# Linear attention and an FFT gate on one Trainium2 core: new shapes for the output transfers, bf16 inverse halves, a new order

## The chip, the core and the metric

The kernel runs on one core of a Trainium2 chip. The core has TensorE (PE) for matrix products into PSUM (8 banks of 2 KB in each of 128 partitions), VectorE (DVE), ScalarE (ACT) and GpSimd (POOL) for elementwise work, and SyncE (SP), which here issues transfers. 16 DMA engines move data between HBM and SBUF; transfers are issued from queues of SP, POOL and, at one place of the new kernel, ACT. The metric is device time in microseconds (us) of one execution.

## What is computed

Batch 8, 8 heads, sequence S = 576, head size 64, model width 512. All inputs and the output are fp32.

```python
kv  = einsum('bhsd,bhse->bhde', k, v)
o   = einsum('bhsd,bhde->bhse', q, kv)
o   = o / sqrt(mean(o*o, axis=-1) + 1e-6) * g_norm
x   = o, heads side by side                     # [8, 576, 512]
x1, x2, x3 = split(x @ w_proj, 3)               # w_proj [512, 1536]
x2_conv = irfft(rfft(x2, axis=1) * rfft(filter_fft, axis=0))   # circular, length 576
out = (x1 * x2_conv * x3) @ w_out               # [8, 576, 512]
```

## The kernel before

The work is written as small steps, each a Python function that issues a few instructions. The string `ORDER` names them one after the other as `step.batch`; each engine runs its own instructions in that order, and waits only for the data and buffers that they need. So the order of the words sets the order on every engine at once, and nothing is reordered later.

For one batch the steps are these.

- *Loads*: `Lq`, `Lk`, `Lv` fetch q, k, v and turn them to bf16 on POOL's queue, double-buffered by batch; `Lw1`, `Lw2`, `Lw3` the three parts of w_proj, `Lwo` w_out, `Lf` the filter. 96 partitions hold six consecutive rows each.
- *Attention*: q is transposed on PE (`T0`, `T1`, evacuated by `eT..`) for the first two batches, and by a DMA transpose on SP's queue (`Qt`) for the others; a tiny POOL copy `one_` then keeps a later load of q behind that transpose. `K`, `eK` make the products k'v and put them in `kvblk`; `O`, `sq`, `ob` (or `ov` on DVE), `R`, `rs` and `x` make the normed x, in 128-channel blocks j with time along the free dimension.
- *Folding and forward transform*: length 576 is split into three thirds and into even and odd parts. `fd`, `fr`, `fa` are the sums and differences of x on DVE; `rrM`, `rrT`, `abM`, `abT` multiply them by the middle third of w_proj; `err`, `eab`, `eT` evacuate to `x2`; `F0`, `F1`, `F2` are the transforms, against tables `FW`, `FX`, `FY`, `FZ`.
- *Product with the filter*: `M0`, `M1`, `M2` on DVE against `HH`, `HM`, then `A0` on POOL and `Av1` on DVE, into `Y`. The tables and `HH`, `HM` are made at the start: `Zi`, `Zt`, `An` the angles, `Tb0` to `Tb2` the transposes, `Ff0` to `Ff2` the folding of the filter, `H0` to `H2`, `HN0`, `HN1` its transform.
- *Gates*: `Ga`, `x1.` (ACT) and `Gb`, `g` (DVE) make x1*x3, four blocks each.
- *Inverse*: for two blocks at a time, `I01`, `I23` the even half and `Io01`, `Io23` the odd half, on PE. ACT copies the odd half to `os` in fp32; DVE combines the even half, straight from PSUM, with it into `u` (`u01`, `u23`). `w` undoes the thirds, `fin` multiplies with the gates into `yg`. The last batch has variants: `J2`, `J3` make whole blocks on PE with the negated table `IVN`, and its thirds are done apart.
- *Output*: `U0`, `U2` multiply two blocks of 128 times of `yg` by w_out, `U4` a block shared by two batches, `V` the last batch's; ACT (`ot0`, `ot2`, `ot4`) evacuates to an `ot` tile, and SP issues the transfers.

PSUM is used as four pairs of banks: `take` gives the pair that has been free longest, also to a step that needs one bank only, and `free` gives it back when its evacuation has been issued. A later step on the same pair waits for that evacuation.

Times are kept in a permuted order: `t_of(blk)` is the first time of a block of 32, whose 32 times lie six rows apart. In 128 partitions of an output block lie four such groups. The kernel issues one transfer for each 32 partitions, often for both blocks of an `ot` tile at once:

```python
return bass.AP(tensor=out.tensor, offset=out.offset + (b * S + t0[0]) * DM, ap=[[6 * DM, 32]] + two + [[1, DM]])
...
for i in range(4):
    nc.sync.dma_start(out=o_rows(b, 2 * (b % 2) + 4 * c0 + i, 2 * (b % 2) + 4 * c0 + 4 + i), in_=ot[32 * i:32 * i + 32])
```

Lines that matter: PE gates L585, output products L708, L721, L747, inverse L612, L613, last batch's inverse L642, L644, half-wide products L505, F2 L552, filter transform L308, L311; DVE product L560, combination L621, L622, x L457; ACT evacuations L522 (x2), L591 (gates), L616 (os), L712 (ot); POOL sum L566; SP transfers L174 (g_norm), L376 (transposes), L715, L728, L762 to L772 (outputs).

Of the kernel before, what the change touches and what calls it, by code (L numbers as in the profile page):

```python
# [19 lines left out]
ORDER = """Lq.0 Z.0 Zi.0 Lkb.0 Lka.0 Zd.0 Zt.0 Lva.0 An.0 Lvb.0 Zf.0 T0.0.18 Act.0 Tb0.0 Lf.0 eTv0.0 Lw1.0 Tb2.0 Tb1.0 Ka.0 eKa.0  # L20
Kb.0 eKb.0 Lq.1 Lw3.0 T1.0 eTv1.0 O01.0 sq1.0 sq0.0 ov1.0 ov0.0 O23.0.2 R0.0 R1.0 Lk.1 sq3.0 sq2.0 rs0.0 ov3.0 ov2.0
R2.0 Lv.1 R3.0 rs1.0 x0.0 Lw2.0 fr0.0 rs2.0 rs3.0 Ff1.0 x1.0 Ff2.0 fd1.0 fr1.0 Ff0.0 T0.1 Ga0.0 eTa0.1 x10.0 Ga2.0
fd0.0 Gb0.0 fa1.0 T1.1 g0.0 eTa1.1 x12.0 H0.0 H2.0 Lv.2 H1.0 K.1 fa0.0 Ga1.0 eK.1 x11.0 HN0.0 rrM.0 O01.1 rrT.0 sq1.1
ob1.1 Lk.2 err.0 sq0.1 abM.0 Gb2.0 ob0.1 F0.0 g2.0 eab.0 abT.0 eT.0 O23.1 F2.0 M0.0 sq2.1 ob2.1 Gb1.0 F1.0 M2.0 sq3.1
HN1.0 ob3.1 R1.1 g1.0 Lq.2 R0.1 Ga3.0 rs1.1 rs0.1 R2.1 K.2 Lq.3 A0.0 Qt.2 M1.0 R3.1 Qt.3 x13.0 rs2.1 x0.1 rs3.1 eK.2
Lk.3 Lv.3 Gb3.0 Av1.0 Io01.0 os01.0 I01.0 x1.1 O01.2 Lwo.0 g3.0 u01.0 Ga1.1 fd.1 sq1.2 Io23.0 ob1.2 R1.2 x11.1 Lv.4
Ga0.1 rs1.2 I23.0 os23.0 fa.1 abM.1 sq0.2 fr.1 x10.1 ob0.2 u23.0 w.0 eab.1 abT.1 O23.2 rrM.1 eT.1 sq3.2 R0.2 rrT.1
ob3.2 rs0.2 fin.0 F2.1 err.1 Gb1.1 sq2.2 F0.1 M2.1 Ga3.1 ob2.2 Lk.4 g1.1 R3.2 Lq.5 x13.1 Lq.4 F1.1 rs3.2 M0.1 K.3 eK.3
R2.2 M1.1 Gb3.1 rs2.2 Gb0.1 g3.1 O23.3 U0.0 sq2.3 sq3.3 x1.2 g0.1 Ga2.1 Av1.1 x0.2 A0.1 ob3.3 ot0.0 Io01.1 x12.1 fd.2
os01.1 fa.2 Gb2.1 I01.1 Io23.1 ob2.3 u01.1 g2.1 Lv.5 abM.2 I23.1 os23.1 abT.2 u23.1 eab.2 eT.2 Ga0.2 x10.2 O01.3 K.4  # L30
Ga1.2 Qt.4 sq0.3 fr.2 ob0.3 eK.4 sq1.3 rrM.2 x11.2 F1.2 w.1 rrT.2 R2.3 ob1.3 err.2 Gb0.2 rs2.3 fin.1 M1.2 F0.2 U2.0
R3.3 g0.2 rs3.3 Gb1.2 M0.2 F2.2 A0.2 ot2.0 g1.2 R0.3 M2.2 R1.3 Ga2.2 rs1.3 Ga3.2 x1.3 rs0.3 x0.3 x12.2 O23.4 Lq.6
x13.2 sq2.4 Av1.2 Gb2.2 ob2.4 U4.1 Lk.5 sq3.4 fd.3 ob3.4 g2.2 ot4.1 U0.1 fa.3 fr.3 Qt.5 R3.4 Io01.2 ot0.1 os01.2 abT.3
rs3.4 I01.2 eT.3 u01.2 Gb3.2 Io23.2 g3.2 os23.2 I23.2 abM.3 u23.2 eab.3 O01.4 rrM.3 F1.3 sq0.4 w.2 ob0.4 sq1.4 rrT.3
err.3 M1.3 U2.1 ob1.4 F0.3 Ga1.3 R1.4 fin.2 ot2.1 x11.3 Ga0.3 Gb0.3 M0.3 R0.4 A0.3 rs1.4 x10.3 Av1.3 F2.3 Lv.6 rs0.4
g0.3 Gb1.3 Zn.0 R2.4 M2.3 rs2.4 g1.3 Lk.6 K.5 Io01.3 I01.3 x1.4 os01.3 x0.4 eK.5 Ga2.3 x12.3 u01.3 Ga3.3 O23.5 Io23.3
x13.3 os23.3 sq3.5 ob3.5 U0.2 ot0.2 fd.4 I23.3 sq2.5 ob2.5 fa.4 Gb2.3 u23.3 Lk.7 g2.3 abM.4 O01.5 fr.4 eab.4 abT.4
Gb3.3 Qt.6 sq0.5 eT.4 ob0.5 sq1.5 rrM.4 g3.3 R3.5 rrT.4 rs3.5 err.4 K.6 F1.4 eK.6 Ga1.4 ob1.5 R0.5 Ga0.4 x11.4 w.3
F0.4 rs0.5 x10.4 fin.3 M1.4 M0.4 F2.4 R1.5 U2.2 rs1.5 Gb1.4 R2.5 M2.4 ot2.2 A0.4 g1.4 Ga3.4 O23.6 rs2.5 x13.4 sq2.6
x1.5 Av1.4 ob2.6 Gb0.4 sq3.6 Gb3.4 ob3.6 g0.4 g3.4 Ga2.4 x12.4 U4.3 x0.5 O01.6 Io01.4 fd.5 ot4.3 sq0.6 U0.3 os01.4  # L40
ob0.6 fr.5 sq1.6 I01.4 Gb2.4 ob1.6 u01.4 Lq.7 rrM.5 Io23.4 Lv.7 ot0.3 R0.6 g2.4 I23.4 rrT.5 os23.4 rs0.6 K.7 fa.5
u23.4 R1.6 abT.5 err.5 abM.5 rs1.6 w.4 R3.6 Qt.7 eT.5 eK.7 eab.5 F0.5 Ga1.5 rs3.6 R2.6 F1.5 x11.5 fin.4 F2.5 rs2.6
M0.5 U2.3 M1.5 A0.5 ot2.3 Ga0.5 x10.5 M2.5 Gb1.5 x1.6 g1.5 Av1.5 O23.7 sq2.7 Gb0.5 Ga2.5 ob2.7 sq3.7 g0.5 Ga3.5 x0.6
x12.5 ob3.7 fd.6 I01.5 fa.6 Gb2.5 Io01.5 x13.5 g2.5 U0.4 Io23.5 os01.5 Ga0.6 u01.5 ot0.4 fr.6 os23.5 I23.5 abM.6 u23.5
abT.6 x10.6 Gb3.5 eab.6 O01.7 eT.6 Ga1.6 w.5 g3.5 sq1.7 F1.6 ob1.7 fin.5 x11.6 sq0.7 rrM.6 R0.7 rrT.6 ob0.7 rs0.7 M1.6
F2.6 R1.7 err.6 M2.6 Gb0.6 rs1.7 F0.6 g0.6 U0.5 R2.7 M0.6 Ga2.6 x0.7 rs2.7 R3.7 x12.6 Gb1.6 Gb2.6 A0.6 ot0.5 rs3.7
Av1.6 g1.6 Ga3.6 g2.6 Io01.6 x1.7 fr.7 I01.6 x13.6 Gb3.6 os01.6 g3.6 Io23.6 u01.6 U2.4 ot2.4 rrM.7 fd.7 fa.7 Ga0.7
I23.6 os23.6 u23.6 x10.7 rrT.7 err.7 abM.7 Ga1.7 w.6 eab.7 abT.7 F0.7 Gb0.7 x11.7 eT.7 Gb1.7 F2.7 fin.6 M0.7 g0.7 F1.7
A0.7 U2.5 M2.7 M1.7 ot2.5 U0.6 Gb2.7 ot0.6 Av1.7 Io01.7 g1.7 I01.7 os01.7 J2.7 uj2.7 Ga2.7 x12.7 u01.7 Ga3.7 w01.7
x13.7 J3.7 g2.7 fin01.7 Gb3.7 uj3.7 wo23.7 U4.5 g3.7 fo23.7 Vp0.7 ot4.5 wm23.7 U4a.7 Vp2.7 Vq0.7 U4b.7 vap0.7 fm23.7  # L50
vau.7 dsp01.7 vvp1.7 Vq2.7 U2.6 dgp12.7 vaq0.7 dgp13.7 vvq1.7 dsp10.7 dgp03.7 dsu0.7 dsu1.7 dsq01.7 dsp00.7 dgu2.7
dsq00.7 dgq02.7 dgp02.7 dsp11.7 dgq03.7 ot2.6 dgu3.7"""
# [769 lines left out]
```

## Time and profile before

| | |
|---|---|
| three runs, median | 223.71 us (221.02 to 224.76) |
| span of the profiled execution | 218.7 us |
| PE busy | 203.8 us, 93% |
| DVE busy | 187.8 us, 86% |
| ACT busy | 147.6 us, 68% |
| POOL busy | 52.0 us, 24% |
| mean granted TensorE clock | 0.993 |
| moved by DMA | 30.12 MB, 138 GB/s |
| output transfers | 68 from `U_ev` and `U4_ev`, 16 for the last blocks |

The span runs from the first to the last instruction of one profiled execution; the median of the separately timed runs is 5.0 us above it. Busy time is the union of an engine's instructions; consecutive matmuls overlap in it, and their ends are modelled. A line of groups reads: source line, engine, operation, output and inputs, shapes, count, then busy us and mean ns, then the idle time ahead of it and what ended it. In the rows on transfers, q0 is POOL's queue and q1 the queue of SP (and of ACT); a packet is what one DMA engine moves at a time.

### The profile page before, as it was taken

How to read it: one execution, taken by the hardware profiler on the slowest of the kernel's cores; microseconds unless marked ns; L12 is line 12 of the kernel's file. 1: busy time of each engine (PE TensorE's matmuls, PEld its weight loads, DVE VectorE, ACT ScalarE, POOL GpSimd, SP SyncE). 2: the span in 40 equal slices, each digit the busy share in tenths (PEclk: the TensorE clock that was granted, in tenths of full speed). 3: DMA queues.
4: the chain of work that ended last, by engine and by line, in shares of the span. 5: the costliest groups of instructions: out<-in, count | busy, mean ns of one | idle time of the engine just before them, and what ended most of it. 6: DMA issues, size and time to landing. Idle time of an engine off the chain costs nothing.

```text
span 218.7 us, 4569 instructions
## 1 busy us (share of the span) xinstructions
PE 203.8 (93%) x1829; PEld 123.3 (56%) x1829; DVE 187.8 (86%) x277; ACT 147.6 (68%) x231; POOL 52.0 (24%) x61
## 2 busy tenths in 40 slices
...
GB/s 41 184 212 202 204 205 204 205 185 71 194 201 204 240 169 63 161 209 180 100 103 199 229 1 165 216 162 27 96 31 67 0 89 34 74 1 167 66 159 188
DMA packets 41032, 30.12 MB, mean 138 GB/s; under 512 B 15986, under 2 KB 36466, under 8 KB 41010
## 3 DMA queue, kind: packets, MB, share of 16 engines
...
HBM read 33.69 MB, written 9.44 MB: 197 GB/s over the span
## 4 chain that ended last, share of the span: by engine, by line
PE 70%; DVE 15%; ACT 7%; POOL 3%; issue 2%; POOLq 0%; DVEq 0%; ACTq 0%
PE ps L585 24%; PE ps L708 10%; PE ps L512 5%; PE ps L612 4%; DVE tpw L560 3%; PE ps L518 2%; PE ps L498 2%; PE ps L429 2%; PE ps L351 2%; PE ps L552 2%; POOL Y L566 2%; PE ps L422 2%; PE ps L544 2%; PE ps L747 2%; PE ps L545 2%
## 5 line engine op out<-in xcount | busy, mean ns | idle before, releaser
L585 PE MATMUL ps<-x,wp 128*128 128x288 bf16 x512 | 71.0, 286 | 0.2
L585 PEld LDWEIGHTS <-wp 128*128 128x128 bf16 x512 | 48.8, 98 | 17.3 <-issue 2.0
L566 POOL TENSOR_TENSOR Y<-tpw 97x1024 bf16<-97x1024 f32 x8 | 21.4, 2670 | 67.7 <-DVE tpw L560 67.7
L560 DVE TENSOR_TENSOR tpw<-ps,HH 97x2048 f32<-97x2048 f32 (+1 forms) x16 | 36.4, 2286 | 1.0 <-PE ps L537 0.4
L443 ACT ACTIVATE rstd<-ps,bias_eps 128x576 bf16<-128x576 f32 x32 | 23.3, 748 | 8.8 <-PE ps L429 8.3
L593 DVE TENSOR_TENSOR g<-ps,x 128x576 bf16<-128x576 f32 x32 | 24.1, 752 | 5.3 <-ACT o L439 3.5
L591 ACT CAST x<-ps 128x576 bf16<-128x576 f32 x32 | 20.5, 640 | 9.4 <-PE ps L585 6.1
L708 PE MATMUL ps<-wo,yg 128*128 128x512 bf16 x112 | 26.3, 379 | 0.0
L522 ACT CAST x<-ps 128x1024 bf16<-128x1024 f32 (+1 forms) x24 | 20.8, 874 | 6.4 <-PE ps L512 4.8
L432 ACT ACTIVATE sq<-ps 128x576 bf16<-128x576 f32 x32 | 20.7, 661 | 2.6 <-PE ps L422 2.6
L712 ACT COPY ot<-ps 128x1024 f32<-128x1024 f32 x12 | 12.2, 1017 | 13.3 <-PE ps L708 13.2
L439 ACT ACTIVATE o<-ps,g_col 128x576 bf16<-128x576 f32 x28 | 21.1, 755 | 0.0
L708 PEld LDWEIGHTS <-yg 128*128 128x128 bf16 x112 | 10.5, 97 | 12.2 <-issue 0.6
L377 POOL COPY one__100<-qT 1x2 bf16<-1x2 bf16 x6 | 2.0, 329 | 64.3 <-DMA qT<-qb 64.3
L612 PE MATMUL ps<-IV,Y 128*128 128x192 bf16 x120 | 15.7, 246 | 0.3 <-DVE Y L566 0.3
L512 PE MATMUL ps<-wp,ab 128*128 128x512 bf16 x64 | 15.1, 379 | 0.0
L621 DVE TENSOR_TENSOR u<-ps,os 128x576 bf16<-128x576 f32 x15 | 11.3, 755 | 3.3 <-PE ps L613 2.3
L616 ACT COPY os<-ps 128x576 f32<-128x576 f32 x15 | 9.6, 641 | 6.1 <-PE ps L613 3.2
L429 PE MATMUL ps<-sq,ind 128*128 128x288 bf16 x64 | 12.6, 286 | 1.1 <-DVE o L437 0.9
L457 DVE TENSOR_TENSOR x<-o,rstd 128x1152 bf16<-128x1152 bf16 x16 | 12.8, 812 | 0.3 <-ACT rstd L443 0.3
L613 PE MATMUL ps<-IV,Y 97*128 97x96 bf16 x60 | 12.4, 207 | 0.2 <-POOL Y L566 0.2
L612 PEld LDWEIGHTS <-Y 128*128 128x128 bf16 x120 | 9.5, 98 | 3.3 <-DVE Y L566 0.6
...
## 6 DMA issues: line engine op xcount, KB each, us to landing
out_dram<-ot SPq DMA_DIRECT2D x50, 128.0 KB, 2.4
...
kb<-in_k_dram POOLq DMA_DIRECT2D x7, 576.0 KB, 11.1
vb<-in_v_dram POOLq DMA_DIRECT2D x7, 576.0 KB, 12.1
wp<-in_moe_w_proj_dram POOLq DMA_DIRECT2D x3, 512.0 KB, 16.6
...
```

The costliest lines, as they stand in the source:

```text
L432: act.activation(out=halves(sq()[:, j]), in_=tmp['o', b, j][:, :, 0:TH], func=AF.Square)
L439: act.activation(out=by_time(osb(), j), in_=i_, func=AF.Copy, scale=g_col)
L443: act.activation(out=by_time(rstd(), j), in_=by_row(tmp['r', b, j]), func=AF.Abs_reciprocal_sqrt, scale=1.0 / D, bias=bias_eps)
L512: nc.tensor.matmul(pp[:, h], abt()[:, j, 2 * h * P:(2 * h + 1) * P], w2(j), start=(j == 0), stop=(j == NDC - 1))
L522: act.copy(out=o_(), in_=tmp[key, b])
L560: vec.tensor_mul(out=t_[:n], in0=xp[:n].unsqueeze(1).to_broadcast([n, 2, 2, DM]), in1=two)
L566: op(out=Yt()[:n, 2 * g:2 * g + 2], in0=t_[:n, ::-1, 0], in1=t_[:n, ::-1, 1])
L585: nc.tensor.matmul(pp[:, h, 0:TH], w_, x[:, j, h * TH:(h + 1) * TH], start=(j == 0), stop=(j == NDC - 1))
L591: act.copy(out=x1, in_=pp[:, :, 0:TH])
L593: vec.tensor_mul(out=halves(g13t()[:, dc]), in0=pp[:, :, 0:TH], in1=x1)
L612: nc.tensor.matmul(pp[:, i, 0:SB], Y[:, 2 * g + h, cs], IV[:, 2 * g + h, 0:SB], start=(g == 1), stop=(g == 2))
L708: nc.tensor.matmul(pp[:, cc], ygt(b)[:, dc, b % 2 * 64 + c * P:b % 2 * 64 + (c + 1) * P], wo[:, dc], start=(dc == 0), stop=(dc == NDC - 1))
```

## The change

- *Outputs.* `t_of` now counts the times of a third in another order (`blk % 6` in place of `blk % 6 // 3 + 2 * (blk % 3)`), so that the four groups of 32 in a block of 128 follow each other by one row. A block whose four groups lie in one third is written by one transfer of 128 partitions, and every third block, which crosses into the next third, by two transfers of 64. `ot` tiles rotate by a table. The last batch has no special transfers; one of its transfers is issued by ACT.
- *Inverse.* ACT evacuates both halves, even and odd, in bf16 into one tile `eo` (`es`, `os`); DVE combines them in SBUF, for all four blocks at once, except in the last batch. `J2`, `J3` and `IVN` are no longer used.
- *Filter transform on full rows.* The third row block of `ff` and `FW` is filled up with zeros, and `H2`'s table is used for both halves at once: six matmuls in place of twelve. The angles are computed with fewer steps, the absolute value on DVE.
- *F2.* Three full matmuls become two pairs of half-wide ones (`FV`).
- *Single banks.* `take` manages eight banks; a step that needs one takes one.
- *Transpose.* POOL's wait for a DMA transpose is a step of its own, `Qh`.
- *Order.* `ORDER` is another string.

```diff
-ORDER = """Lq.0 Z.0 Zi.0 Lkb.0 Lka.0 Zd.0 Zt.0 Lva.0 An.0 Lvb.0 Zf.0 T0.0.18 Act.0 Tb0.0 Lf.0 eTv0.0 Lw1.0 Tb2.0 Tb1.0 Ka.0 eKa.0
+ORDER = """Z.0 W.0.16 Lqa.0 Zi.0 Zt.0 An.0 Zd.0 Zf.0 T0.0 eTv0.0 Zz.0 Tb2.0 Tb1.0 Tb0.0 Lf.0 Ff1.0 Ff0.0 Ff2.0 Lvb.0 Lkb.0 Kb.0
...
-        i = min(range(4), key=lambda x: seen[x])
+        idle = [x for x in range(8) if seen[x] is not None]
+        if n == 2:
+            i = min((x for x in idle if x % 2 == 0 and x + 1 in idle), key=lambda x: max(seen[x], seen[x + 1]))
+        else:
+            i = min(idle, key=lambda x: (x ^ 1 in idle, seen[x]))
...
-        return SB * (blk // 6) + blk % 6 // 3 + 2 * (blk % 3)
+        return SB * (blk // 6) + blk % 6
...
-                m = P if a < 2 else 32
-                kw = dict(start=(a == 0), stop=(a == 2))
-                if g < 2:
-                    nc.tensor.matmul(hp[:n, ri], FW[:m, a, 2 * g + ri, 0:n], ff[:m, a, ri], **kw)
-                else:
-                    for dup in range(2):
-                        nc.tensor.matmul(hp[dup * NM:(dup + 1) * NM, ri], FW[:m, a, 4 + ri, ri * NM:(ri + 1) * NM], ff[:m, a, ri], **kw)
+                nc.tensor.matmul(hp[:n, ri], FW[:, a, 2 * g + ri, 0:n], ff[:, a, ri], start=(a == 0), stop=(a == 2))
...
     def by_time(t, j):
-        return t[:, j].rearrange("p (m a r) -> p a m r", m=3, a=2)
+        return t[:, j].rearrange("p (m a r) -> p a m r", m=9, a=2)
...
-        for i in range(3):
-            mm(xp, FZ[:, 2 + i], x2[:, 2 + i], start=(i == 0), stop=(i == 2))
+        for c, t_ in ((lo, FW[:, 0, 4, lo]), (hi, FV)):
+            mm(xp[c], t_, x2[:, 2 + c.start // 64], start=True, stop=False, tile_position=(0, c.start))
+        for c in (lo, hi):
+            mm(xp[c], FZ[:, 2, c], x2[:, 4], start=False, stop=True, tile_position=(0, c.start))
...
-    def inv_os(b, d0):
-        act.copy(out=buf("os", 0, [P, 2, TH], FP32), in_=tmp['i', b, d0, 1][:, :, 0:TH])
-        free(("i", b, d0, 1))
-
-    def inv_u(b, d0):
-        p_, os_, u = tmp['i', b, d0, 0][:, :, 0:TH], buf("os", 0, [P, 2, TH], FP32), ut()[:, d0:d0 + 2]
-        vec.tensor_add(out=u[:, :, 0:TH], in0=p_, in1=os_)
-        vec.tensor_sub(out=u[:, :, TH:S], in0=p_[:, :, ::-1], in1=os_[:, :, ::-1])
-        free(("i", b, d0, 0))
+    eo = lambda: buf("eo", 0, [P, 2, NDC, TH])
+
+    def inv_ev(b, d0, h):
+        act.copy(out=eo()[:, h, d0:d0 + 2], in_=tmp['i', b, d0, h][:, :, 0:TH])
+        free(("i", b, d0, h))
+
+    def inv_u(b, d0, n):
+        e_, o_ = (eo()[:, h, d0:d0 + n] for h in range(2))
+        u = ut()[:, d0:d0 + n]
+        vec.tensor_add(out=u[:, :, 0:TH], in0=e_, in1=o_)
+        vec.tensor_sub(out=u[:, :, TH:S], in0=e_[:, :, ::-1], in1=o_[:, :, ::-1])
...
+    def o_rows(b, g, n=1):
+        return bass.AP(tensor=out.tensor, offset=out.offset + (b * S + SB * (g // 3) + 2 * (g % 3)) * DM,
+                       ap=[[DM, 2 * n], [6 * DM, 32], [1, DM]])
+
+    def o_dma(q, b, blk, t):
+        if blk % 3 != 2:
+            q.dma_start(out=o_rows(b, blk, 2), in_=t)
+        else:
+            for i, r in enumerate((lo, hi)):
+                q.dma_start(out=o_rows(b, blk + i), in_=t[r])
...
     def U_ev(b, c0):
-        ot = ot_tile(b)
+        ot = ot_tile(b, c0)
         act.copy(out=ot, in_=tmp['u', b, c0])
         free(("u", b, c0))
-        for i in range(4):
-            nc.sync.dma_start(out=o_rows(b, 2 * (b % 2) + 4 * c0 + i, 2 * (b % 2) + 4 * c0 + 4 + i), in_=ot[32 * i:32 * i + 32])
+        for i in range(2):
+            o_dma(nc.sync, b, b % 2 + 2 * (c0 + i), ot[:, i])
...
+    def V(b, c):
+        for h in range(1 if c < 3 else 2):
+            n = DM if c < 3 else DM // 2
+            tmp['v', c, h] = take(("v", c, h), 1)
+            for dc in range(NDC):
+                nc.tensor.matmul(tmp['v', c, h][:, 0:n], ygt(b)[:, dc, 64 + c * P:64 + (c + 1) * P], wo[:, dc, h * n:(h + 1) * n],
+                                 start=(dc == 0), stop=(dc == NDC - 1))
```

What the change moves on the queues is seen in the built programs' orders (line, operation, output and input, shape of the output). On SP's queue, the last rows before, from the last transpose on; `ot`, `sq`, `o` and `rstd` are the tiles that hold output blocks:

```order
L376 DMA_TRANSPOSE qT<-qb_75 128x24x96
L715 DMA out_dram<-ot 32x2x512 x2
L715 DMA out_dram<-ot 64x1x512 x4
L715 DMA out_dram<-ot 32x2x512 x12
L715 DMA out_dram<-ot 64x1x512 x2
L715 DMA out_dram<-sq 64x1x512 x2
L715 DMA out_dram<-sq 32x2x512 x2
L728 DMA out_dram<-ot 32x512 x4
L762 DMA out_dram<-ot 32x512 x2
L772 DMA out_dram<-o 32x512 x2
```

The same place after the change:

```order
L714 DMA out_dram<-ot 4x32x512
L717 DMA out_dram<-ot 2x32x512 x2
L714 DMA out_dram<-ot 4x32x512 x3
L717 DMA out_dram<-ot 2x32x512 x2
L714 DMA out_dram<-o 4x32x512 x2
L714 DMA out_dram<-sq 4x32x512
L717 DMA out_dram<-sq 2x32x512 x2
L717 DMA out_dram<-rstd 2x32x512 x2
L714 DMA out_dram<-ot 4x32x512
L717 DMA out_dram<-ot 2x32x512 x2
L714 DMA out_dram<-ot 4x32x512
```

Transfers of 32 partitions and two blocks, or 32 partitions, have become transfers of 128 partitions with an outer size of 4, and pairs of 64 partitions with an outer size of 2; the number of rows of 2 KB is the same.

On ACT, around the first inverse after batch 1's k'v (`x` is a gate or an x2 evacuation, `rstd`, `sq`, `o` the attention), before:

```order
L591 CAST x_564<-ps_67 128x576
L443 ACTIVATE rstd<-ps_68,bias_eps 128x2x3x96
L616 COPY os<-ps_69 128x576
L432 ACTIVATE sq<-ps_66 128x576
L591 CAST x_427<-ps_67 128x576
L439 ACTIVATE o<-ps_66,g_col 128x2x3x96
L522 CAST x_586<-ps_69 128x1024
```

and after:

```order
L608 CAST x_661<-ps_66 128x576
L635 CAST eo<-ps_69 128x576
L635 CAST eo<-ps_67 128x576
L608 CAST x_582<-ps_66 128x576
L635 CAST eo<-ps_69 128x576
L608 CAST x_661<-ps_67 128x576
L635 CAST eo<-ps_66 128x576
```

ACT now has four evacuations of the inverse where it had two (the second `os` comes further down), and they stand close together.

On POOL's queue, the first loads before (`kb`, `vb`, `qb` with two buffers each, `fn` the filter, `wp` the parts of w_proj in the order w1, w3, w2):

```order
L120 DMA qb_74<-in_q_dram 96x8x384
L178 ISA
L178 IOTA ki 128x1
L180 IOTA tvi 128x384
L120 DMA kb_70<-in_k_dram 96x4x384 x2
masks.py:197 MEMSET ident 128x128
masks.py:199 AFFINE_SELECT ident<-ident 128x128
L120 DMA vb_72<-in_v_dram 96x4x384 x2
L278 DMA fn<-in_moe_filter_fft_dram 96x3072
L129 DMA wp<-in_moe_w_proj_dram 128x4x512
L120 DMA qb_75<-in_q_dram 96x8x384
```

and after, from the filter on (the first half of q stands ahead of it; `wp` comes as w2, w1, w3):

```order
L298 DMA fn<-in_moe_filter_fft_dram 96x3072
L126 DMA vb_72<-in_v_dram 96x4x384
L126 DMA kb_70<-in_k_dram 96x4x384 x2
L126 DMA vb_72<-in_v_dram 96x4x384
L126 DMA qb_74<-in_q_dram 96x4x384
L126 DMA qb_75<-in_q_dram 96x8x384
L126 DMA kb_71<-in_k_dram 96x8x384
L126 DMA vb_73<-in_v_dram 96x8x384
L135 DMA wp<-in_moe_w_proj_dram 128x4x512
L126 DMA vb_72<-in_v_dram 96x8x384
L135 DMA wp<-in_moe_w_proj_dram 128x4x512
```

The filter now comes second, and the first part of w_proj after batch 1's q, k and v.

232 lines of the change are left out of this document (107 added, 125 removed).

## The prediction

> **What bounds the kernel now.** I read the page first, then the engines stretch by stretch, then the tail in order of time, then the transfers.
>
> ```profile
> span 218.7 us, 4569 instructions
> PE 203.8 (93%) x1829; PEld 123.3 (56%) x1829; DVE 187.8 (86%) x277; ACT 147.6 (68%) x231; POOL 52.0 (24%) x61
> ```
>
> The stretches (columns: PE, weight loads, DVE, ACT and POOL busy, granted clock, transfer share, GB/s) say where:
>
> ```profile
> 24.00:30.00 6.00, 6.00 (x53) 3.68 (x50) 5.00 (x12) 2.56 (x4) 0.77 (x1) 1.00 1.31 203
> 60.00:80.00 20.00, 19.93 (x235) 12.83 (x232) 19.47 (x25) 14.88 (x27) 3.12 (x2) 1.00 1.34 212
> 100.00:120.00 20.00, 20.00 (x194) 12.63 (x193) 18.23 (x22) 16.26 (x26) 5.71 (x5) 1.00 0.78 137
> 140.00:160.00 20.00, 20.00 (x191) 13.10 (x189) 19.40 (x24) 14.14 (x22) 2.54 (x2) 1.00 0.55 104
> 180.00:200.00 20.00, 20.00 (x142) 12.36 (x140) 18.89 (x24) 8.65 (x11) 2.36 (x1) 1.00 0.24 59
> 212.00:218.70 6.70, 0.00 (x0) 0.00 (x0) 0.00 (x0) 0.00 (x0) 1.19 (x3) 0.79 0.66 196
> ```
>
> From about 24 to 209 us TensorE never waits, with DVE close behind (18.2 to 19.5 of 20 us). Work taken from DVE or put on ACT is therefore hidden, as long as PE stays fed. The tail is different:
>
> ```profile
> 209.01 1.89 PE L708 MATMUL ps<-wo,yg 128*128 128x512 bf16 x8
> 212.75 0.58 SPq L762 DMA_DIRECT2D out_dram<-ot  x1
> 213.43 2.25 SPq L715 DMA_DIRECT2D out_dram<-rstd  x4
> ```
>
> The last matmul ends at 210.9 and the span 7.8 us later: SP is still issuing transfers until 215.7, about 0.6 us each, and 3.0 us pass from its last issue to the end.
>
> **The transfers, seen closely.** SP's first transfers and what its queue (q1) moved in the first 40 us, in which g_col is its only transfer:
>
> ```profile
> 0.74 0.73 SPq L174 DMA_DIRECT2D g_col<-in_g_norm_dram  x1
> 42.89 6.70 SPq L376 DMA_TRANSPOSE qT<-qb  x2
> ```
> ```profile
> q1 hardware_dynamic: 130, 0.00, 0.1%
> g_col<-in_g_norm_dram SPq DMA_DIRECT2D x1, 0.5 KB
> ```
>
> And from 176 to 190 us, when only outputs move (slices of 0.35 us):
>
> ```profile
> GB/s 0 0 0 0 0 0 41 217 193 193 252 375 199 100 0 0 0 0 0 0 0 0 0 0 0 0 70 205 199 187 281 351 193 12 0 0 0 0 0 0
> DMA packets 642, 1.07 MB, mean 77 GB/s; under 512 B 128, under 2 KB 128, under 8 KB 640
> q1 hardware_dynamic: 640, 1.05, 29.3%
> out_dram<-ot SPq DMA_DIRECT2D x8, 128.0 KB, 2.2
> ```
>
> Eight outputs of 128 KB are 512 packets of 2 KB, and 128 tiny ones are left over: 16 a transfer. g_col is 128 elements of 4 bytes in 130 packets: 2 left over. I read the tiny packets as completions, one from each DMA engine that worked: 16 engines carry an output, 2 carried g_col. The pattern fits the shapes: an output's outermost dimension is 32 rows in both source and target, while g_col's source is [2, 64]. The width is then the largest number up to 16 that divides both outermost sizes.
>
> The new outputs are written as `[[DM, 2n], [6*DM, 32], [1, DM]]`: outermost 4 with 128 partitions on the other side, or 2 with 64. By this reading they run on 4 engines or on 2, where the old ones ran on 16. The Trainium skill, "DMA: Bandwidth & Descriptors", section "Why a DMA increments its semaphore by 16 and not by 1", states the same rule (the largest count up to 16 that divides the slowest dimension of both patterns, and on this queue the lowest-numbered engines); the trace agrees with its counts, 16 and 2, and no row here shows which engines. By that rule the sum is the one I forecast; without it the sum is the first rival's.
>
> **The change, part by part.**
>
> *PE work.* Rows of the chain, in order of time:
>
> ```profile
> 29.34 1.79 PE ps L311 x12
> 80.07 0.55 PE ps L505 x4
> 85.56 0.66 PE ps L552 x3
> 199.38 0.33 PE ps L642 x4
> ```
> ```profile
> L612 PE MATMUL ps<-IV,Y 128*128 128x192 bf16 x120 | 15.7, 246 | 0.3 <-DVE Y L566 0.3
> L311 PE MATMUL ps<-ff,FW 128*64 128x512 bf16 x8 | 1.2, 391 | 0.0
> ```
>
> H2 goes from twelve half-wide matmuls (1.79) to six of 0.66/3 = 0.22: -0.5. F2 goes from three full ones (0.66) to four half-wide like L505 (0.55), eight times: -0.9. The last batch's J2, J3 (four groups like L642, 1.32, and eight small ones) become half as many: -0.8. Sum -2.2, all on the path, since PE is the path.
>
> *DVE and ACT.*
>
> ```profile
> L621 DVE TENSOR_TENSOR u<-ps,os 128x576 bf16<-128x576 f32 x15 | 11.3, 755 | 3.3 <-PE ps L613 2.3 <-ACT os L616 0.8
> L457 DVE TENSOR_TENSOR x<-o,rstd 128x1152 bf16<-128x1152 bf16 x16 | 12.8, 812 | 0.3 <-ACT rstd L443 0.3
> L616 ACT COPY os<-ps 128x576 f32<-128x576 f32 x15 | 9.6, 641 | 6.1 <-PE ps L613 3.2 <-DVE u L622 2.7
> ```
>
> The four half-batch combinations from PSUM (0.755 each, 3.0 a batch) become two over 1152 bf16 elements, priced like L457 (0.81): -1.4 a batch, -11 in all. ACT gains two evacuations of 0.64 a batch, +10. Both lie under PE: 0 to the sum. If PE's cover is gone, ACT's 16.3 of 20 us (100 to 120) becomes 17.5 and still fits. The 32-element runs that `by_time` and `by_row` now have are in no row; between 0 and 0.1 us on 64 evacuations, off the path: 0.
>
> *The start.* Loads land at 203 GB/s (row 24 to 30), 2.9 us for 576 KB, one behind the other.
>
> ```profile
> 8.93 0.54 PEld L385 LDWEIGHTS <-qb 96*128 96x128 bf16 x12 [0.79 <-DMA qb<-in_q_dram]
> 24.04 3.11 PE L585 MATMUL ps<-x,wp 128*128 128x288 bf16 x24
> 29.38 1.11 ACT L319 ACTIVATE hu<-ps,cf 97x1024 f32<-97x1024 f32 x1 [0.30 <-PE ps L308]
> 30.53 1.41 DVE L324 SCALAR_TENSOR_TENSOR HH<-ps,cf,hu 97x512 f32<-97x512 f32 x2 [1.46 <-ACT hu L319]
> 36.50 1.90 PE L512 MATMUL ps<-wp,ab 128*128 128x512 bf16 x8
> ```
>
> The first q landed at 8.9, so the stream began near 6.0. w1 used to end the first 2.9 MB of it (about 20) and now ends 5.8 MB, at 6.0 + 28.4 = 34.4: the gates of batch 0, which began at 24.0, begin ten us later. In exchange the filter transform and the attention come first. Their DVE chain, added up: the last fold is evacuated near 14.2, then eKb and Zc (1.7), hu of H1 at 16.6, three pairs of L324 (4.2), kvblk and three qT copies (2.6), four `ov` (3.0), and x, fr, fd, fa of batch 0 (6.1): 32.5, after which abM.0 can run, which ran at 36.5. One part is later and the other earlier; adding PE's pieces in both orders, I find about 24.5 us of work behind it at 42 us either way. I take 0, with -5 (PE does all that the loads allow) and +3 (every hand-over between engines late) as bounds. The split Qt/Qh only lets POOL issue loads while a transpose is under way: 0.
>
> *Outputs.* 68 issues by `U_ev` and `U4_ev` and 16 at the end become 48, so SP no longer holds the tail; if they kept 16 engines, about 5.5 us would pass from the last matmul to the end instead of 7.8: -2.3. But on 4 or 2 engines each of the 48 puts 32 packets of 2 KB on the busiest engine, where an old 128 KB transfer put 4. The best slice above, 375 GB/s over 16 engines, is 87 ns a packet; the loads' 203 GB/s of bf16 reads twice that in fp32, which as a rate is 80 ns; the 29.3% of 16 engines over 14 us, over 512 packets, is 128 ns. I take 87, from the densest stream of outputs: 2.8 us a transfer. That the engines are the same ones each time is my choice; no row shows it.
>
> Now the queue. Behind U2.4 the order has 24 transfers and, by the pieces above (14 gates at 0.98, five U at 1.73, six single blocks at 0.86, the inverses and transforms of batches 6 and 7), 38.7 us of PE work. The transfers need 24 x 2.8 = 67 us. PE would end at 210.9 - 2.2 = 208.7, so U2.4 is evacuated at 208.7 - 38.7 + 1.0 = 171.0. Between ot0.1 and there, 84 us, the same engines carry 21 transfers (59), ten loads (29) and three transposes (3.4 each): 98 us, 14 over. Loads and outputs overlap in part, and three `ot` tiles let ACT run ahead, so I add 4 (0 to 14). Behind the late transfer waits `U_ev` on ACT for a free `ot` tile, and behind it every evacuation, so PE stops too. End: 171.0 + 4 + 67 + 3.0 = 245 us of span, against 218.7. The runs' median is 223.71, 5.0 above the profiled span (the shown runs 2.3 to 6.1): 250.
>
> **The rivals.**
> - *The outputs stay wide, or their engines change from one to the next.* For it: the old transfers always left 16 completions, and g_col is a single case with tiny elements. Against it: nothing but the outer sizes sets g_col apart. Then 218.7 - 2.2 - 2.3 + 5.0 = 219.2. This is the other side: the change does what it says, and it decides if a 256 KB transfer leaves 16 completions, or if its 4 engines are others than the last one's.
> - *ACT becomes the bound instead.* PSUM pairs of the inverse are now all freed by ACT; if PE waits for each of the 16 added evacuations, 16 x 0.64 = 10 us: 229. Against it: ACT's 3.7 us of slack in 20.
>
> **How the numbers follow.** Narrow outputs on the same engines 0.74 (250), wide or spread 0.18 (219), ACT-bound 0.08 (229). Faster and slower mean by over 2%, about what a measurement of this kernel tells from no change: below 219.2, above 228.2. The first rival falls on both sides of 219.2: faster 0.09, same 0.10, slower 0.81. The likeliest case's own range is 238 (80 ns, nothing late before U2.4) to 275 (about 105 ns, all 14 us late; 128 ns would give 290, but contains contention). To leave out no more than 2 in 10, the range reaches down to 219.
>
> **What would show it.** Right: output transfers with 4 or 2 completions instead of 16; issue to landing of 3 us and far more, in place of 2.2; ACT's `ot` evacuations waiting for outputs; PE done early and a tail of tens of us with a transfer share near 4/16. PE's busy time falls by about 2 us, DVE's by 11, ACT's rises by 10, whichever case holds. Wrong: 16 completions a transfer, or landings near 2.5 us in a full queue. Then the time is near 219. Gaps in PE at 40 to 60 us that end on ACT evacuations would speak for the last rival or a late start.

## The result, and the profile after

The changed kernel takes 279.51 us (median of 4 runs, 278.14 to 280.63), the kernel before on the same chip 222.44 us (221.02 to 224.76): a ratio of 1.255 [1.245, 1.265]. The forecast was 250.0 us with a range of 219 to 275. The direction and the mechanism are there, the time is 29.5 us above the forecast and outside the range. In the experiments below, executions that came out more than 1.5% above the fastest of their kernel are left out of the medians.

The first two lines of the page of the changed kernel, and its stretches (PE, weight loads, DVE, ACT, POOL busy, granted clock, transfer share, GB/s), the same ones as before and then the tail:

```profile
span 276.4 us, 4473 instructions
PE 212.7 (77%) x1800; PEld 126.7 (46%) x1819; DVE 181.7 (66%) x267; ACT 155.7 (56%) x245; POOL 48.4 (18%) x54
```
```profile
24.00:30.00 6.00, 5.16 (x52) 2.90 (x51) 5.13 (x7) 4.35 (x8) 0.41 (x1) 0.50 1.29 204
60.00:80.00 20.00, 18.14 (x173) 11.87 (x173) 16.33 (x20) 13.48 (x23) 2.78 (x1) 1.00 0.99 106
100.00:120.00 20.00, 12.97 (x136) 7.87 (x138) 13.09 (x14) 8.95 (x16) 4.65 (x4) 0.97 0.95 170
140.00:160.00 20.00, 16.54 (x154) 9.69 (x154) 11.36 (x14) 12.68 (x21) 2.48 (x2) 0.93 1.06 127
180.00:200.00 20.00, 19.89 (x160) 13.03 (x161) 17.65 (x22) 15.93 (x27) 3.10 (x3) 1.00 0.20 65
252.00:276.40 24.40, 0.00 (x0) 0.00 (x0) 0.33 (x1) 0.00 (x0) 0.00 (x0) 0.57 0.18 62
```

TensorE was busy throughout before; now 13 to 16.5 of 20 us between 100 and 160, half clock at 24 to 30, and nothing from 252 on. The tail, in order of time (start, us, engine, line, operation); the first row is U2.4's output:

```profile
205.91 1.15 SPq L714 DMA_DIRECT2D out_dram<-ot  x2
...
249.56 1.90 PE L772 MATMUL ps<-wo,yg 128*128 128x512 bf16 x12 [0.84 <-DVE ot L777]
...
252.55 9.55 SPq L717 DMA_DIRECT2D out_dram<-ot  x2
262.63 1.98 SPq L714 DMA_DIRECT2D out_dram<-ot  x1
```

The last matmul ends at 251.5, the span 25 us later. SP needs 9.55 us for two issues where it took some 0.6 us for one. The transfer share and SP's queue from 244 to 248 us:

```profile
DMA  2322332233223322332233223322232223222322
...
q1 hardware_dynamic: 207, 0.41, 26.3%
```

The same queue from 262 to 264 us, where the outputs of 128 KB issued at 252.55 run:

```profile
q1 hardware_dynamic: 52, 0.10, 13.2%
```

And, from the page, ACT's queue, which issues one output of 256 KB in the whole span:

```profile
q10 hardware_dynamic: 132, 0.26, 0.3%
```

132 packets are 128 of 2 KB and 4 completions: 4 engines. A share of 26.3% is 4.2 of 16 engines, 13.2% is 2.1: 4 engines at first and 2 in the end, as forecast for the two shapes. 26.3% of 16 engines in 4 us are 16.8 us, over 199 packets of 2 KB 85 ns each; the forecast had 87.

So the drain is as forecast, and what is not is its start: U2.4 goes out at 205.9 instead of 175. The chain of waits between 100 and 206 (start, us, what) has the longest piece there:

```profile
113.90 2.34 POOL Y L583
116.23 21.64 issue
138.41 0.79 POOL qb L126
139.20 0.75 POOL kb L126
139.95 18.29 DMA vb<-in_v_dram
158.38 0.95 PE ps L363 x48
```

For 21.6 us POOL stands in `Qh`, which waits for a transpose on SP's queue; only then does it issue loads, and v lands 18.3 us later. The first 8.8 us of the piece pass before the transpose is even issued, at 125.0: the q that it turns was issued by POOL at 104.2 and lands only at 124.9. This is a loop: transpose, load, next transpose. For v itself TensorE's `K` waits just 2.4 us. The longest single wait of TensorE in this kernel is another one, 9.0 us for an evacuation by ACT, which itself waits 10.1 us for an `ot` tile whose earlier output isn't through (waits of the changed kernel; us in total, times, longest):

```profile
PE ps L363 <- DMA vb<-in_v_dram: 2.4, 1, 2.4
PE ps L602 <- ACT ot L741: 9.0, 1, 9.0
ACT ot L741 <- DMA out_dram<-ot: 13.3, 2, 10.1
```

Which of the two counts, the loop or the tile, run 6 tells.

### The profile page after: what moved, and what is told of

Its sections match the earlier page's. It is cut to its first block, busy times and chain, and to the rows that moved or that the text cites. A ratio compares the mean times of both kernels' runs of the same rounds, so it can differ in the third digit from the quotient of the medians.

```text
span 276.4 us, 4473 instructions
## 1 busy us (share of the span) xinstructions
PE 212.7 (77%) x1800; PEld 126.7 (46%) x1819; DVE 181.7 (66%) x267; ACT 155.7 (56%) x245; POOL 48.4 (18%) x54
## 3 DMA queue, kind: packets, MB, share of 16 engines
q1 hardware_dynamic: 18766, 12.72, 24.7%
## 4 chain that ended last, share of the span: by engine, by line
PE 46%; DMA 22%; issue 9%; DVE 8%; POOL 3%; ACT 2%; SPq 0%; DVEq 0%; POOLq 0%; ACTq 0%
PE ps L602 17%; DMA vb<-in_v_dram 7%; DMA qb<-in_q_dram 6%; DMA out_dram<-ot 5%; PE ps L737 5%; DMA qT<-qb 4%; PE ps L527 4%; DVE tpw L577 3%; PE ps L629 2%; PE ps L444 2%; PE ps L533 2%; PE ps L513 2%; PE ps L363 2%; PE ps L437 2%; PE ps L520 1%
## 5 line engine op out<-in xcount | busy, mean ns | idle before, releaser
L602 PE MATMUL ps<-x,wp 128*128 128x288 bf16 x512 | 73.0, 295 | 9.0 <-ACT ot L741 9.0
L602 PEld LDWEIGHTS <-wp 128*128 128x128 bf16 x512 | 49.7, 100 | 28.6 <-issue 14.1
L610 DVE TENSOR_TENSOR g<-ps,x 128x576 bf16<-128x576 f32 x32 | 23.8, 755 | 26.5 <-PE ps L602 24.4
L608 ACT CAST x<-ps 128x576 bf16<-128x576 f32 x32 | 20.5, 640 | 15.3 <-PE ps L602 9.3
L737 PE MATMUL ps<-wo,yg 128*128 128x512 bf16 x105 | 27.6, 398 | 0.4
L447 ACT ACTIVATE sq<-ps 128x576 bf16<-128x576 f32 x32 | 20.4, 656 | 11.5 <-PE ps L437 11.2
L454 ACT ACTIVATE o<-ps,g_col 128x576 bf16<-128x576 f32 x28 | 20.7, 748 | 0.0
L635 ACT CAST eo<-ps 128x576 bf16<-128x576 f32 x32 | 18.9, 655 | 2.1 <-PE ps L630 2.1
L737 PEld LDWEIGHTS <-yg 128*128 128x128 bf16 x112 | 11.2, 101 | 12.6 <-issue 2.1
L527 PE MATMUL ps<-wp,ab 128*128 128x512 bf16 x62 | 16.5, 408 | 0.1
L444 PE MATMUL ps<-sq,ind 128*128 128x288 bf16 x64 | 14.3, 314 | 0.8 <-DVE o L452 0.7
L369 ACT CAST kvblk<-ps 64x256 bf16<-64x256 f32 (+2 forms) x25 | 8.8, 350 | 9.8 <-PE ps L363 8.4
L437 PE MATMUL ps<-qT,kvblk 64*64 64x288 bf16 x128 | 8.7, 341 | 7.2 <-DMA qT<-qb 6.4
L630 PE MATMUL ps<-IV,Y 97*128 97x96 bf16 x64 | 13.2, 207 | 0.0
L472 DVE TENSOR_TENSOR x<-o,rstd 128x1152 bf16<-128x1152 bf16 x16 | 11.9, 751 | 2.0 <-ACT rstd L458 1.9
L363 PE MATMUL ps<-vb,kb 96*64 96x64 bf16 x384 | 8.3, 202 | 6.3 <-DVE Y L592 3.3
```

Source lines behind the costliest of these rows:

```text
L447: act.activation(out=halves(sq()[:, j]), in_=tmp['o', b, j][:, :, 0:TH], func=AF.Square)
L454: act.activation(out=by_time(osb(), j), in_=i_, func=AF.Copy, scale=g_col)
L527: nc.tensor.matmul(pp[:, h], abt()[:, j, 2 * h * P:(2 * h + 1) * P], w2(j), start=(j == 0), stop=(j == NDC - 1))
L602: nc.tensor.matmul(pp[:, h, 0:TH], w_, x[:, j, h * TH:(h + 1) * TH], start=(j == 0), stop=(j == NDC - 1))
L608: act.copy(out=x1, in_=pp[:, :, 0:TH])
L610: vec.tensor_mul(out=halves(g13t()[:, dc]), in0=pp[:, :, 0:TH], in1=x1)
```

## The experiments

Times below are medians, each beside runs of the kernel before on the same chip (medians of 221.1 to 223.1 us). "U2.4" is the time at which U2.4's first output is issued in the profiled execution; behind it the same work is left in all of them.

**1. Wide outputs, all else as changed.**

```diff
-        for i in range(2):
-            o_dma(nc.sync, b, b % 2 + 2 * (c0 + i), ot[:, i])
+        for i in range(4):
+            x = 2 * (b % 2) + 4 * c0 + i
+            nc.sync.dma_start(out=o_blk(b, x, x + 4), in_=ot[32 * i:32 * i + 32])
```

(`o_blk` is before's `o_rows`; the blocks of U4 and V likewise.)

> The changed kernel with its outputs in the shape of before: 32 partitions a transfer, outermost size 32, 84 transfers for 48; all else as changed. Theory N (the outputs' outermost size of 4 or 2 puts them on 4 or 2 engines, and that alone makes the kernel slow, by the drain at the end and by holding up loads and transposes before it): 16 completions a transfer, the evacuation of U2.4 back from 206 us to 175-180, time 219 to 228. Theory O (the new order and the late loads of the start make U2.4 late, and the narrow outputs only the drain behind it): U2.4 stays at 200 or later, and with 39 us of TensorE work behind it the time is 245 to 255. Theory A (ACT, with its added evacuations, is the bound): about 229, with TensorE waiting for ACT at evacuations of the inverse.

Measured 237.43 us, ratio 1.069 [1.059, 1.080]; U2.4 at 185.5, last matmul at 225.1. An output of 128 KB is again 64 packets and 16 completions (four of them: 320 packets). The shape alone costs 279.5 - 237.4 = 42.1 us. But theory N's 219 to 228 is missed too: the wide twin is 14 us slower than the kernel before, so something besides the outputs is at fault. Its row on ACT and on TensorE at the largest wait:

```profile
126.00 1.01 ACT L746 COPY ot<-ps 128x1024 f32<-128x1024 f32 x1 [5.36 <-DMA out_dram<-ot]
127.06 0.48 PE L629 MATMUL ps<-IV,Y 128*128 128x192 bf16 x2 [4.91 <-ACT ot L746]
```

**2. The kernel before, its U outputs narrow.**

```diff
-            nc.sync.dma_start(out=o_rows(b, ...), in_=ot[32 * i:32 * i + 32])
+            x = 2 * (b % 2) + 4 * (c0 + i % 2) + i // 2 * 2
+            nc.sync.dma_start(out=o_two(b, x), in_=ot[i // 2 * 64:i // 2 * 64 + 64, i % 2])
```

> The kernel before with the 60 transfers of its U evacuations in another shape alone: the same count and the same 128 KB each, but 64 partitions of 2 KB with outermost size 2 instead of 32 partitions of 4 KB with 32 (of some pairs of blocks the two are swapped in the output). Theory N: 2 completions a transfer, each 32 packets of 84 ns on the busiest engine = 2.7 us, so 60 take 161 us behind the first one at 69.9: a span of at least 234, a time of 239 or more, up to 290 with the loads held up. Theories O and A: nothing of the change's order is in it, so 220 to 226.

288.33 us, 1.302 [1.290, 1.313]: same count, same bytes, same order, 65 us more, TensorE busy for only 9.5 of 20 us at 140 to 160. (Of some pairs of blocks the two are swapped in the output; the bytes moved are the same.) The narrow shape suffices, without anything else of the change. The edit also doubles the partitions of a transfer, 64 for 32; that 64 or 128 partitions alone do no harm to outputs isn't tried.

**3 and 4. Narrow only behind U2.4, narrow only ahead of it.**

```diff
+    late = lambda: clock[0] > ORDER.split().index("U2.4")
...
+        if late():
+            for i in range(2):
+                o_dma(nc.sync, b, b % 2 + 2 * (c0 + i), ot[:, i])
+        for i in range(0 if late() else 4):
...
```

> The changed kernel with its outputs wide as in the first run up to U2.4, and narrow as changed from U2.4 on: it takes away what narrow outputs do to the first part and leaves the drain. Theory N: U2.4 evacuated near 175-180 as in the first run, 24 transfers of 2.7 us behind it (65 us) and 3: span 243 to 250, time 247 to 254. Theory O: U2.4 still near 206, time 275 to 280.

> The reverse of the run before: narrow as changed up to U2.4, wide from U2.4 on. It leaves what narrow outputs do to loads, transposes and evacuations and takes the drain away. Theory N: U2.4 stays near 206, and what follows is TensorE's 39 us of work and about 6 us of tail: span near 250, time 250 to 256. Were the narrow outputs harmless ahead of U2.4 (they only drain late), and the start at fault: the same. If both are harmless and the 31 us come of a full queue at the end alone: 222 to 230.

(In the second, `late` has `<=` for `>`.) Run 3: 258.37, 1.166 [1.151, 1.180], U2.4 at 187.2, span end 68.7 us later. Run 4: 257.01, 1.159 [1.139, 1.179], U2.4 at 208.5 (in an execution of 261.93). Against the wide twin the late half costs 20.9 us and the early half 19.6; together 40.5, against 42.1 for both. The cost has two halves of about the same size, which nearly add; the forecast had sized the early half at 4.

**5 and 6. Output tiles in the order of use, wide and narrow.** The change hands out the `ot` tiles by `kept[b, c] % 3`, that is by batch number. In the new order ot4.1 and ot0.2, neighbours, get the same tile.

```diff
+        used.setdefault((b, c), len(used))
...
-        return buf("ot", kept[b, c] % 3, [P, 2, DM], FP32)
+        return buf("ot", used[b, c] % 3, [P, 2, DM], FP32)
```

> The first run (the changed kernel with wide outputs, 237.4 us) with one more edit: the three output tiles are handed out in the order in which the evacuations come, as before, not by batch number (which gives one tile to ot0.0 and ot0.1, to ot2.0 and ot2.1, to ot4.1 and ot0.2, each pair one behind the other in the order). Theory T (the new handing out of the tiles makes one evacuation wait for the output of the one just ahead of it; the first run shows 6.5 us of it at 119 to 126 on ACT and 4.9 on TensorE): that wait goes, time 230 to 234. Theory S (loads and transposes set that stretch, the wait only takes their place): 235.5 or more.

> The changed kernel, outputs narrow as it has them, with the tiles handed out in the order of use as in the run above. Theory T: a narrow output holds its tile for 3 to 12 us longer, so that the waits of 13.3 us of ACT's evacuations, and the 10.0 us of TensorE behind them, are a large part of the 20 us by which narrow outputs make U2.4 late; time 262 to 272. Theory Q (loads and transposes stand behind the outputs on the four engines, whichever tile): 275 or more.

Wide: 230.64, 1.035 [1.027, 1.044], U2.4 at 178.4; theory T holds, 6.8 us. Narrow: 278.20, 1.244 [1.235, 1.252], U2.4 at 205.5: nothing. Theory Q's number. ACT's wait for the tile, the 10.1 us above, is gone there, but TensorE has others in its place (waits of the narrow kernel with tiles in turn; us in total, times, longest):

```profile
PE ps L437 <- DMA qT<-qb: 11.4, 2, 8.3
PE ps L363 <- DMA vb<-in_v_dram: 9.2, 1, 9.2
```

So with the tile's wait gone the loop still holds U2.4 at the same time; the tile only stood in front of it.

**7. PSUM in pairs again** (`take` as before, on the wide twin).

```diff
-            i = min(idle, key=lambda x: (x ^ 1 in idle, seen[x]))
...
+        i = min((x for x in range(0, 8, 2) if seen[x] is not None), key=lambda x: seen[x])
+        held[key] = [i, i + 1]
```

> The first run with PSUM handed out in pairs as before, no single banks. Theory B (a key that takes one bank takes the other half of a pair that is in use, whose last reader has hardly begun: the three waits of 3.3 us of K on the products of F2): those waits go, time 233 to 236. Rival: with fewer pieces other steps wait for a pair, 238 or more.

No verdict: four executions from 229.15 to 237.59. In the profiled one the waits of `K` are gone, and so is the wait for the `ot` tile, which nothing in the edit touches. It is tried again in 14.

**8. Idle matmuls in the start** (on the wide twin).

```diff
-... T1.0 eTv1.0 ... O01.0 ... R3.0 ... R0.0 ... K.1 ... rrM.0
+... T1.0.6 eTv1.0 ... O01.0.3 ... R3.0.4 ... R0.0.3 ... K.1.2 ... rrM.0.3
```

> The first run with idle matmuls of 0.21 us (at full clock) between 20 and 35 us, where TensorE waits for loads and DVE and the granted clock falls to 0.63 and 0.69 (6 ahead of T1.0, 3 of O01.0, 4 of R3.0, 3 of R0.0, 2 of K.1, 3 of rrM.0): the price of the cold stretch. Theory C (the low clock there adds some 3.6 us to the matmuls of the start): time 234 to 236. Theory D (DVE's chain of 16 us from 17.8 on and the loads set the start, whatever the clock): 237 to 239.

236.11, 1.059 [1.053, 1.066]: between the two theories, 1.3 us. The granted clock from 20 to 40 us is 0.91 instead of 0.66, but U2.4 is still at 185.7, since the wait for the `ot` tile takes it up (6.0 us in place of 4.9).

**9 and 10. Transposes on TensorE, narrow and wide.**

```diff
-... Qt.5 ot4.1 O23.5 ...
+... ot4.1 T0.5 eTv0.5 T1.5 eTa1.5 O23.5 ...
```

Batches 2 to 7 are done alike, and without `Qh`; batch 5 is shown. In both, TensorE's transposes of batch 4 come behind the load of batch 6 into the same buffer, so batch 4 is computed with the q of batch 6.

> The changed kernel, outputs narrow, but the q of batches 2 to 7 transposed on TensorE (as batches 0 and 1 are) instead of by transposes on SP's queue, and without POOL's wait for them: nothing but outputs is left on SP's queue. It costs TensorE some 1.4 us and DVE 1.4 a batch. Theory Qt (the transposes stand behind narrow outputs on SP's queue: 9 to 10 us each where they take 3 to 4, and POOL's loads stand behind them): U2.4 comes 10 to 20 us earlier than at 206, time 262 to 275, and it is further from its wide twin, the next run, by less than 42 us. Theory L (the loads themselves are slowed by sharing the four engines, and ot tiles): U2.4 at 204 or later, time 278 or more, 42 us or more above the twin.

> The twin of the run above with wide outputs: what the transposes on TensorE cost by themselves against the first run's 237.4. All theories: 232 to 246, the added 8 us of TensorE against waits for transposes that go.

278.67, 1.253 [1.244, 1.263], U2.4 at 207.1; the twin 253.96, 1.143 [1.134, 1.151], U2.4 at 200.9, beyond what was expected of it, because `O` now waits for the evacuations of its own transposes. The twins are 24.7 us apart, and 6.3 at U2.4, instead of 42.1 and 20.4. With no transposes among the transfers, narrow outputs hold up the first part by a third as much; a kernel that is late anyway has more room to hide it, so this is no clean price.

**11. Narrow outputs issued by POOL.**

```diff
-            o_dma(nc.sync, b, b % 2 + 2 * (c0 + i), ot[:, i])
+            o_dma(nc.gpsimd, b, b % 2 + 2 * (c0 + i), ot[:, i])
```

> The changed kernel, the outputs in its own shape, but every one issued by POOL instead of SP (and ACT): is the width a matter of the shape alone, or of the queue too? Theory N as it stood (shape alone): 4 or 2 completions a transfer, time 275 or more, with loads behind outputs on POOL. Rival (POOL's queue spreads packets over all 16 engines, as its loads do): landings near 3 us, the transfer share in the tail above 0.5, time 232 to 255.

307.86, 1.385 [1.372, 1.399], from two executions. The time is the first case's. Of the rival the spread holds: the transfer share of the last 21 us (slices of 0.5 us, in tenths) goes far above 4/16,

```profile
DMA  1696595976787666545433413945355423210000
```

so on this queue outputs of the same shape do not stay on the same four engines. Landings near 3 us do not: the outputs land 8.1 us (256 KB) and 7.7 us (128 KB) after their issue, by the medians of the page. The loads stand behind outputs on POOL, and `K` waits 23.8 us for k and 9.1 for v; that is where the time shows. The Trainium skill, "DMA: Bandwidth & Descriptors", section "Why a DMA increments its semaphore by 16 and not by 1", says that the software queue puts narrow transfers on consecutive engines from a cursor that moves on, and the hardware queue on the lowest-numbered ones; run 11 fits the first, the changed kernel's share near 4/16 the second; which numbers the engines have no run shows.

**12 and 13. Transposes issued by ACT, narrow and wide.**

```diff
-        nc.sync.dma_start_transpose(...)
+        nc.scalar.dma_start_transpose(...)
```

> The changed kernel with one word changed: the six transposes are issued by ACT, the outputs stay narrow on SP, so that a transpose no longer stands in one queue behind them. Theory F (that standing in one queue is most of the 20 us by which narrow outputs make U2.4 late: 206 against 185.5 in the first run): U2.4's outputs issued within 8 us of those of the next run, its wide twin; a transpose takes 3 to 5 us. Theory E (it is the four engines that they share, whatever the queue; or the loads): the twins stay 15 us or more apart at U2.4.

> The twin with wide outputs: the first run (237.4) with the transposes issued by ACT, which spends about 3 us on issuing each. Both theories: 235 to 250.

289.83, 1.307 [1.299, 1.314], U2.4 at 218.8; wide 254.48, 1.148 [1.140, 1.156], above the 235 to 250 expected, U2.4 at 201.7. The twins are 17.1 us apart at U2.4: theory F falls. Standing in one queue is not most of it. That it is the engines shared with the outputs is what is left of the two theories, and no run shows it apart from the rest. The loads do get later: v, issued third in its group, lands after 20.7 us in the narrow one, 12.6 in the wide one.

**14 to 17. What is left: pairs, tail, start.** All on wide outputs with tiles in the order of use. 14 adds PSUM in pairs; 15 also deals the last blocks' outputs to SP and POOL in turn; 16 adds the idle matmuls of run 8 (the texts on 14, 15 and 17 call it the mended kernel); 17 deals those of U0.6 and U4.7 to POOL too and one block to ACT.

```diff
-q_=q_: [q_.dma_start(out=o_blk(b, 2 + 4 * c + i), ...
+q_=q_: [(nc.sync, nc.gpsimd)[i % 2].dma_start(out=o_blk(b, 2 + 4 * c + i), ...
```

> Wide outputs, tiles in the order of use, PSUM in pairs; without the idle matmuls and the shared tail of the mended kernel (222.5). Theory B (single banks cost 3.3 us in three waits of K): 226 to 229 against 230.6 with single banks. Rival: 230 to 232, pairs bring nothing.

> The run above with the last blocks' outputs issued by SP and POOL in turn, that is the mended kernel without the idle matmuls. If the tail is worth 3 to 5 us: 222 to 225, and what is left to 222.5 is the price of the cold start (0 to 2).

> The changed kernel with four edits: wide outputs, tiles in the order of use, PSUM in pairs, the idle matmuls of the start, and the last blocks' outputs issued by SP and POOL in turn. By the single results: 230.6 with wide outputs and tiles in turn, less 2 to 4 for the waits of K, 0 to 4 for the start, 3 to 5 for the tail of 11 us from the last matmul to the end: 218 to 226. If the start and the order cost what nothing of this touches, 226 to 231.

> The mended kernel (222.5, same as before) with the outputs of its last four groups dealt to three queues: U0.6 to POOL, half of U4.7 and of two last blocks to POOL, one block to ACT, the rest to SP. In the mended kernel TensorE ends at 215.2 and SP issues until 220.0; with the issues done by 217.3 and 3 us behind the last one, the span falls by 2 to 3 us: time 219 to 221, ratio 0.982 to 0.995 to before. If it is the transfers themselves that fill the tail (28 of them, 2.6 MB, at up to 375 GB/s 7 us), nothing: 222 to 223.

The line of 15 and 16 is shown. 14: 229.96, 1.040 [1.031, 1.049], nothing against run 5's 1.035, though `K`'s waits of 3.3 us are gone and U2.4 is at 175.2. But its profile is of an execution of 227.4 us whose granted clock from 20 to 40 us was 0.91, with nothing to keep it up; in runs 5 and 15 it was 0.66. Run 15, with pairs too, has U2.4 at 176.5, so of the 3.2 us against run 5 the pairs bring 1.9 at the same clock. 15: 224.51, 1.014 [1.008, 1.020]: the tail is worth 5.5 us by the times, and by the profiles 7.2 us instead of 11.4 pass from the last matmul to the end. 16: 222.49, 1.002 [0.997, 1.007], the same as the kernel before. 17: 222.96, 1.008 [1.003, 1.014]: a miss; 8.0 us still pass from the last matmul (212.9) to the end (220.9). SP was to be done by 217.3 and issued until 218.3, 2.6 us before the end. Whether the issues or the transfers fill that tail stays open; no run took any of the transfers away. No version beats the kernel before. Page of 16:

```profile
span 222.5 us, 4589 instructions
PE 205.3 (92%) x1840; PEld 123.5 (56%) x1840; DVE 181.6 (82%) x267; ACT 154.7 (70%) x245; POOL 54.2 (24%) x62
```

## Why the prediction was wrong in its size

*The width: right.* The rule read from 130 and 640 packets held for 4 and for 2, and run 2 shows that the narrow shape costs that much without the rest of the change.

*Packet price and drain: right.* 85 ns against 87; behind U2.4 67 + 3.0 = 70 us were forecast, and 276.4 - 205.9 = 70.5 passed. In run 3 it was 68.7. "The same engines each time" was a choice; the share of 26.3%, which stays near 4/16 with many outputs queued, and run 11 bear it out for SP's queue. TensorE's work behind U2.4, 38.7 by the sum, is 225.1 - 185.5 = 39.6 in run 1.

*The 4 us ahead of U2.4: the step that failed, and with it the 0 for the start.* The forecast said "Loads and outputs overlap in part, and three `ot` tiles let ACT run ahead, so I add 4 (0 to 14)", and took 0 for the start. Its 175 was 205.9, 30.9 us late; with 0.5 more for the drain, and a median that stands 3.1 above the span instead of 5.0, that is the whole error of 29.5. From its 171.0, the sum without these 4 us, 205.9 is 34.9 us off, and the wide twin splits them in two:

- *14.5 us that are there with wide outputs as well* (185.5 - 171.0). Of these 7.1 are the `ot` tiles handed out by batch (run 5). The forecast counted three tiles and did not look at which evacuation gets which; `kept` stood in the diff. 1.9 more go with PSUM in pairs in the profiles (178.4 to 176.5, runs 5 and 15), a difference that the times don't resolve. The rest, 5.5 us, lies at the start and in the order. From 20 to 40 us run 1's granted clock is 0.66 (0.58 in the changed kernel, 1.00 before), and TensorE waits there in short pieces for q's load, ACT and DVE; for w2 it does not wait. By 42 us it has done some 3 to 4 us less of matmuls than before (an estimate: the matmuls of both traces up to there, idle ones left out, 512 columns at 0.22 us), where the forecast found the start equal. The warm start brought about 2 us in run 16 against 15. The split is not exact: with tiles in turn in both (runs 6 and 5) narrow outputs make U2.4 27.1 us later, not 20.4, since in the narrow kernel the wait for the tile was hidden.
- *20.4 us that narrow outputs add ahead of U2.4.* The term added up what the four engines carry, as if it were one queue with 14 us too much. It left out that the load and transpose steps form a loop, each waiting for the last: POOL's `Qh` holds the loads until the transpose is through, and the transpose needs the load. In the forecast's words, "The split Qt/Qh only lets POOL issue loads while a transpose is under way: 0". A pass round it is lengthened twice, by the load and by the transpose. SP's transposes, changed kernel, then wide twin (start, us):

```profile
71.44 13.08 SPq L388 DMA_TRANSPOSE qT<-qb  x2
125.00 9.28 SPq L388 DMA_TRANSPOSE qT<-qb  x1
153.00 12.41 SPq L388 DMA_TRANSPOSE qT<-qb  x2
```
```profile
68.84 6.78 SPq L388 DMA_TRANSPOSE qT<-qb  x2
110.22 3.41 SPq L388 DMA_TRANSPOSE qT<-qb  x1
136.72 5.91 SPq L388 DMA_TRANSPOSE qT<-qb  x2
```

About 6 us more each time. The load of q that the middle one waits for, with the time from issue to landing at the end of the row, changed, then wide:

```profile
qb<-in_q_dram POOLq DMA_DIRECT2D x1, 576.0 KB, 20.7
```
```profile
qb<-in_q_dram POOLq DMA_DIRECT2D x1, 576.0 KB, 13.0
```

And the three last loads, changed, then wide:

```profile
qb<-in_q_dram POOLq DMA_DIRECT2D x1, 576.0 KB, 8.9
kb<-in_k_dram POOLq DMA_DIRECT2D x1, 576.0 KB, 11.8
vb<-in_v_dram POOLq DMA_DIRECT2D x1, 576.0 KB, 18.3
```
```profile
qb<-in_q_dram POOLq DMA_DIRECT2D x1, 576.0 KB, 6.7
kb<-in_k_dram POOLq DMA_DIRECT2D x1, 576.0 KB, 9.5
vb<-in_v_dram POOLq DMA_DIRECT2D x1, 576.0 KB, 11.5
```

In this pass q lands 7.7 us later after its issue, POOL goes on 13.0 us after that landing instead of 5.1, and v lands 6.8 us later after its issue. POOL's waits for the transposes, changed, then wide:

```profile
POOL one__102 L392 <- DMA qT<-qb: 26.0, 2, 21.7
POOL qb L126 <- DMA qT<-qb: 15.2, 1, 15.2
```
```profile
POOL one__102 L392 <- DMA qT<-qb: 11.7, 2, 6.1
POOL qb L126 <- DMA qT<-qb: 9.0, 1, 9.0
```

20.5 us more of it; that this comes near the 20.4 proves nothing, for TensorE feels only part of POOL's waits. The transposes at 153.0 (136.7), for one, wait for TensorE, not for their load, which had landed at 147.3 in the changed kernel. Transposes and loads both get later (the rows above, runs 12 and 13), and without transposes on SP's queue a gap of 6.3 us is left (runs 9 and 10); how the 20.4 us divide between them stays open, since each run that takes one away shifts the other.

*Work moved between engines: right, and without effect.* DVE's combinations fell from 22.5 to 12.4 us (forecast -11),

```profile
L641 DVE TENSOR_TENSOR u<-eo 128x1152 bf16<-128x1152 bf16 (+1 forms) x9 | 6.2, 689 | 2.7 <-ACT eo L635 2.3
L642 DVE TENSOR_TENSOR u<-eo 128x1152 bf16<-128x1152 bf16 (+1 forms) x9 | 6.2, 685 | 0.0
```

DVE as a whole by 6.1, since other rows grew; ACT rose by 8.1 (forecast 10). TensorE's -2.2 can't be read from the changed kernel, which runs partly at a low clock; in run 16, without the idle matmuls, TensorE is busy for about 194.2 us (205.3 less 11.1) against 196.2 before (203.8 less 7.6), some 2 us less, and the time is the same.

*The rivals.* The wide one gave 219.2; run 1 took 237.4, with the 14.5 us above and a tail of 10.9 us instead of 5.5, for wide again means 84 issues. The sum for this rival lacked the same 14.5 us as the forecast. ACT as the bound: no wait on an `eo` evacuation stands among run 1's larger ones; it fell.
